# Infini-attention and GEGLU on one core: four stack tiles of a kind in place of five, two slots more, another order

## The chip, the cores and the metric

The kernel runs on one core of a Trainium2 chip. A core has engines that each work through a queue of their own, in order: TensorE (PE, matrix products, with its weight loads, PEld), VectorE (DVE), ScalarE (ACT), GpSimd (POOL), and SyncE (SP), which here issues nearly all transfers (DMA). They wait for each other by semaphores. Products are written to PSUM, eight banks of 128 partitions by 512 floats; everything else lives in SBUF or in DRAM.

The metric is the device time of one execution in microseconds (us), as the median of several runs. A verdict of faster or slower is given at 2%.

## The reference, cut

`x` is 2048 rows of 512 floats. Attention has 32 heads of 16 columns, in four segments of 512 rows; a memory `M`, `z` is carried from segment to segment. Then comes a feed-forward part of width 1376. All is float32.

```python
def _A_ref(x, wq, wk, wv, wo, beta):
    ...
    for s in range(N):                                   # N = 4 segments
        qs, ks, vs = q[:, :, s], k[:, :, s], v[:, :, s]
        logits = einsum("bhqd,bhkd->bhqk", qs, ks) * scale + mask   # causal
        a_dot = einsum("bhqk,bhkd->bhqd", softmax(logits), vs)
        pq = phi(qs)                                     # t > 0 ? t + 1 : exp(t)
        num, den = pq @ M, pq @ z + 1e-6
        outs.append(g * num / den + (1.0 - g) * a_dot)   # g = sigmoid(beta), one per head
        pk = phi(ks)
        M, z = M + pk.T @ vs, z + sum(pk)
    return concat(outs) @ wo

def _B_ref(x, w_gate, w_up, w_down):
    return (gelu(x @ w_gate) * (x @ w_up)) @ w_down

h  = x + _A_ref(layernorm(x), wq, wk, wv, wo, beta)
h2 = h + _B_ref(layernorm(h), w_gate, w_up, w_down)
```

## The kernel before

**Two halves of each number.** Operands of the large products are split into a high part in the PE's rounded format and the rest, and three products of the parts stand for one (`SPLIT`). A tile with both parts is [128, 2, 512] and is called a *slot*. Slots hold split weights (`split_weight`, `split_wv`), the transposed normalized rows, the projections before they are spread out (`hls` in `qkv`), the attention's output, and in the feed-forward part its weights and activations. One pool, `S4`, has 18 of them.

**Units and stacks.** The attention works by 16 units U, each a group of eight heads (`c`) in a segment (`s`); each unit has two halves, Q = 2U and 2U + 1, so Q runs from 0 to 31. `qkv(U)` projects q and k for a unit (`project`, L932), writes high and low part to a slot (ACT L1043, DVE L1045), and copies them with six transfers per half, three for q and three for k, into the *stacks*: a tile `stq` and a tile `stk` for each Q, in which every head takes four rows (lines 1056 and 1062 issue the copies). In a stack of K, a row of ones remains from the fill; in a stack of Q, one row of each four holds zeros at first, and later the row maxima that `pass_a` finds.

`pass_a(Q)` multiplies Q by K for the row maxima (PE L1186, DVE L1196), turns them and writes them into the stack (transfer at L1224). `pass_b(Q)` multiplies again (L1244), takes the exponential on ACT (L1250), masks on POOL (L1258) and multiplies by V (`accum`, L1272). After the last L1244 of a Q its two stacks are free. They come from pools that hand out tiles in the order of the units, five of each kind:

```python
S4 = Pool_(slots("slot", 18))
stk_t = slots("stk", 5)
PSK = Pool_(stk_t, fifo=True, then=S4)
stq_t = slots("stq", 5)
PSQ = Pool_(stq_t, fifo=True, then=S4)
```

`then=S4` says that a stack that no later Q needs becomes a slot. So 28 tiles of this size are shared by all.

Stacks are filled once on POOL: those of Q with zeros (`c_fill`, L645), those of K with ones (`c_stk`, L660). The first five Q take tiles that were so filled; from the sixth on, a transfer of 16 KB (`dst.t[3:P:32]` from `amask`, L1069) clears the row that the maxima of the tile's last user were in.

**PE's three ways of working.** Products of q, k and of most of the attention use 64 rows of the array at a time, two at once (mode "r" in the code); products by V and those with the memory use 32 columns, four at once (mode "c"); the first projection and the feed-forward part use the whole array (mode "f").

**After the attention** each segment's output is multiplied by `wo` (L1352 for two segments, L1345 for two) and normalized (`ln2`), and the feed-forward part runs in two passes of 1024 rows over 11 blocks of its width: `ffn` (L1531, activations in `geglu`) and `down` (L1596, added up by DVE at L1604). In `geglu` the low half of the result is made by POOL, and for block 9 by DVE (L1563).

**The order.** Every operation is recorded by `Sched.op` with the engine that runs it, its reads and writes, and is numbered as it is recorded. `Sched.run(ORDER)` then emits them in the sequence of a list, `ORDER`, one number for each operation. The list sets the order on each engine's queue, and which tile each value gets: a pool gives the tile that comes free first by the planner's estimate. A later operation on an engine never passes an earlier one.

At the start, POOL fills a stack, makes the identity (L629 to L633) and later the iotas of the head mask (L612, L616). PE warms up with 14 transposes (L869) once the identity and the first rows are there; then come the transposes of the first segment (L894), the first projection (L953), and V's (L994).

Of the kernel before, what the change touches and what calls it, by code (L numbers as in the profile page):

```python
# [7 lines left out]
F32 = mybir.dt.float32  # L8
# [48 lines left out]
    76, 0, 5, 9, 6, 1, 10, 12, 4, 7, 13, 14, 8, 16, 27, 11, 91, 18, 92, 88, 93, 15, 17, 89, 19, 77, 28, 94, 29,  # L57
    167, 30, 25, 90, 21, 23, 20, 31, 102, 821, 33, 97, 46, 822, 47, 103, 104, 32, 95, 22, 34, 825, 44, 87, 35,
    36, 24, 168, 105, 37, 42, 106, 164, 107, 110, 826, 38, 108, 827, 40, 96, 26, 82, 111, 100, 43, 828, 84, 98,
    39, 41, 109, 118, 128, 45, 81, 824, 48, 51, 50, 829, 119, 165, 830, 831, 112, 130, 99, 113, 823, 129, 114,  # L60
    115, 1608, 116, 117, 133, 134, 78, 120, 140, 121, 122, 49, 138, 169, 166, 52, 832, 124, 53, 123, 139, 144,
    127, 833, 834, 2, 835, 54, 135, 85, 55, 75, 131, 3, 132, 145, 1026, 146, 136, 137, 147, 150, 149, 148, 170,
    56, 181, 58, 253, 172, 634, 1024, 186, 254, 255, 151, 171, 256, 59, 57, 176, 1028, 184, 185, 188, 126, 182,
    190, 125, 187, 101, 141, 142, 189, 152, 257, 154, 74, 162, 143, 183, 153, 177, 179, 60, 836, 258, 178, 173,
    61, 180, 1029, 175, 67, 68, 1025, 174, 837, 62, 63, 191, 625, 192, 259, 631, 65, 64, 69, 260, 79, 70, 66,
    193, 194, 195, 197, 71, 72, 198, 632, 261, 73, 213, 214, 262, 161, 270, 196, 263, 838, 272, 199, 273, 438,
    2986, 628, 158, 264, 268, 839, 439, 267, 239, 240, 241, 242, 440, 215, 243, 274, 269, 271, 229, 230, 232,
    276, 441, 840, 86, 275, 233, 442, 217, 216, 203, 224, 227, 225, 228, 226, 277, 266, 443, 231, 279, 234, 265,
    83, 237, 204, 235, 238, 205, 206, 236, 444, 1030, 841, 278, 200, 202, 445, 157, 1031, 207, 245, 842, 446,
    248, 449, 208, 246, 201, 843, 209, 450, 212, 448, 211, 633, 210, 244, 249, 247, 635, 218, 155, 250, 280,  # L70
    447, 1032, 219, 220, 221, 844, 222, 163, 845, 156, 846, 251, 847, 292, 848, 1033, 849, 295, 406, 286, 1034,
    407, 281, 296, 287, 852, 1035, 223, 282, 293, 297, 288, 408, 299, 318, 850, 300, 298, 301, 409, 410, 283,
    319, 80, 289, 321, 294, 328, 291, 329, 290, 302, 1027, 411, 304, 636, 303, 306, 313, 159, 331, 305, 307,
    412, 316, 314, 361, 362, 363, 364, 365, 323, 308, 324, 326, 626, 332, 317, 413, 320, 353, 354, 355, 366,
    367, 368, 369, 370, 414, 327, 797, 322, 818, 1036, 315, 427, 428, 1417, 309, 310, 330, 815, 311, 312, 798,
    415, 432, 325, 434, 627, 356, 357, 358, 359, 360, 433, 252, 417, 418, 799, 416, 334, 335, 421, 422, 800,
    419, 801, 337, 333, 338, 336, 284, 339, 429, 430, 431, 420, 629, 630, 387, 1037, 285, 340, 390, 391, 350,
    351, 352, 371, 372, 388, 802, 377, 160, 380, 378, 379, 803, 392, 435, 398, 393, 395, 425, 804, 401, 436,
    396, 373, 375, 341, 374, 376, 437, 805, 399, 809, 482, 483, 484, 485, 486, 426, 808, 586, 342, 424, 806,
    389, 477, 478, 479, 480, 481, 394, 423, 587, 1038, 807, 382, 383, 384, 343, 1411, 381, 402, 2122, 466, 467,  # L80
    468, 588, 514, 385, 386, 515, 516, 517, 589, 344, 819, 1039, 345, 346, 503, 506, 504, 469, 470, 471, 397,
    493, 590, 472, 473, 474, 475, 476, 603, 607, 400, 591, 494, 496, 498, 592, 508, 820, 499, 501, 495, 511,
    505, 593, 541, 542, 497, 487, 347, 509, 543, 594, 816, 488, 781, 500, 544, 545, 518, 536, 512, 540, 608,
    510, 2113, 538, 489, 490, 507, 491, 492, 595, 1040, 609, 403, 502, 457, 539, 537, 614, 615, 596, 513, 519,
    1224, 613, 610, 458, 611, 404, 1041, 533, 1225, 612, 597, 520, 598, 1042, 817, 578, 600, 581, 602, 601, 534,
    521, 405, 535, 599, 1226, 567, 530, 579, 570, 568, 1227, 562, 571, 606, 563, 565, 546, 531, 1228, 532, 547,
    616, 1229, 548, 572, 580, 564, 573, 618, 604, 575, 348, 550, 649, 549, 582, 551, 552, 651, 617, 1230, 557,
    650, 560, 558, 1043, 767, 662, 664, 768, 553, 665, 555, 663, 554, 1231, 1420, 666, 522, 646, 648, 1418, 605,
    1232, 576, 657, 647, 661, 574, 660, 769, 652, 556, 659, 1233, 770, 1235, 656, 459, 1234, 658, 771, 566,
    1236, 654, 673, 851, 1414, 1044, 561, 1045, 569, 653, 674, 559, 577, 676, 583, 584, 683, 655, 772, 460, 524,  # L90
    525, 688, 773, 684, 678, 675, 677, 774, 686, 1046, 689, 1047, 667, 691, 685, 668, 681, 669, 1048, 679, 1049,
    1050, 1051, 1052, 727, 671, 690, 728, 729, 731, 670, 349, 775, 730, 776, 692, 694, 777, 461, 680, 717, 672,
    695, 718, 697, 779, 526, 721, 719, 786, 787, 792, 791, 795, 788, 687, 682, 693, 793, 720, 780, 637, 698,
    696, 699, 451, 462, 789, 700, 453, 778, 796, 638, 722, 790, 724, 723, 853, 1609, 726, 463, 464, 465, 989,
    452, 738, 701, 990, 794, 725, 585, 739, 741, 714, 743, 715, 744, 716, 746, 991, 753, 756, 1054, 740, 711,
    992, 619, 713, 993, 745, 742, 871, 527, 523, 873, 784, 872, 1003, 754, 755, 712, 994, 759, 621, 1419, 783,
    995, 879, 1056, 762, 620, 880, 760, 732, 782, 748, 749, 881, 751, 882, 996, 874, 702, 2119, 733, 875, 734,
    736, 735, 757, 876, 997, 737, 750, 883, 998, 854, 877, 752, 747, 855, 878, 1010, 999, 884, 1011, 785, 761,
    887, 528, 758, 1191, 885, 886, 1610, 763, 888, 868, 856, 1008, 1009, 869, 1012, 1053, 859, 639, 1192, 1004,
    1000, 703, 860, 622, 764, 1421, 857, 1055, 623, 765, 870, 858, 1193, 895, 1007, 898, 899, 1194, 1013, 896,  # L100
    897, 1195, 949, 1422, 950, 1006, 952, 910, 1018, 889, 913, 914, 951, 911, 890, 912, 1014, 953, 1001, 529,
    1017, 900, 901, 1015, 902, 704, 1196, 1002, 903, 904, 905, 705, 936, 908, 909, 906, 907, 1197, 1005, 1016,
    916, 919, 938, 1198, 917, 937, 918, 944, 891, 945, 892, 948, 946, 893, 947, 894, 1199, 1200, 861, 939, 862,
    1201, 810, 1213, 920, 863, 940, 941, 811, 1214, 454, 812, 1202, 864, 455, 866, 943, 1215, 706, 915, 766,
    865, 813, 867, 942, 1412, 707, 1216, 921, 922, 1203, 923, 814, 1217, 1082, 1083, 1586, 1084, 1086, 1219,
    1085, 975, 1204, 1587, 976, 977, 1218, 624, 978, 979, 933, 708, 934, 1588, 960, 961, 962, 963, 964, 935,
    954, 1205, 924, 955, 1589, 981, 1087, 982, 1208, 984, 709, 1605, 965, 966, 967, 968, 969, 1590, 1207, 1090,
    1089, 1591, 1088, 970, 1222, 971, 972, 973, 974, 1091, 1071, 1073, 1072, 1592, 1077, 1078, 1079, 956, 957,
    958, 926, 1080, 1220, 1593, 1221, 1206, 1074, 1146, 1081, 1075, 1594, 927, 1150, 1076, 1149, 1147, 1415,
    1597, 983, 1413, 1148, 985, 980, 1596, 1092, 1243, 959, 986, 1598, 1093, 1094, 1595, 1141, 987, 1095, 1096,  # L110
    1223, 925, 1209, 1019, 1020, 456, 1244, 1210, 640, 1021, 1245, 1113, 1116, 1142, 1143, 1372, 1145, 1117,
    1144, 1114, 1108, 1135, 1111, 1137, 988, 1136, 1373, 1097, 1416, 1098, 1268, 1109, 1271, 1099, 1212, 1270,
    1374, 710, 1211, 1272, 1119, 1269, 928, 1375, 1101, 1103, 641, 1120, 1376, 1121, 1122, 1102, 1104, 1138,
    1377, 642, 643, 1139, 1162, 1123, 1106, 1606, 1378, 1140, 644, 1165, 1151, 645, 1163, 1100, 1152, 1105,
    1107, 929, 1607, 1389, 1167, 1112, 1379, 1170, 2995, 1110, 1115, 1172, 1168, 1153, 1171, 1154, 1169, 1255,
    1166, 1164, 1380, 1175, 1155, 1258, 1257, 1256, 1383, 1173, 1259, 1384, 1118, 1381, 1394, 1260, 1156, 1157,
    1158, 1177, 1261, 2989, 1174, 1159, 1160, 1385, 1124, 1161, 1176, 1382, 1246, 1262, 1180, 1125, 1181, 1252,
    1126, 1253, 1057, 1058, 1183, 1391, 1392, 1178, 1393, 1179, 1254, 1396, 1022, 930, 1184, 2307, 1186, 1023,
    1059, 1263, 1395, 1127, 1387, 1294, 1397, 1187, 1295, 1185, 1266, 1182, 1267, 1296, 1060, 3183, 1297, 1062,
# [1579 lines left out]
```

## Time and profile before

| | |
|---|---|
| median of 3 runs | 746.7 us (745.68 to 749.15) |
| the profiled execution | 746.94 us, of which its span is 745.2 us |
| granted TensorE clock in it | 1.0 |
| transfers | 107.92 MB, 145 GB/s on average |

The span goes from the first to the last instruction. A row of the list of groups gives line, engine, operation, output and inputs by tile name, shape and count, then busy time and mean length, then the idle time of the engine just before, with what ended it. A row of a timeline gives start and length, and [idle time and what ended it] where the engine had waited. PE's lengths overlap, since its products are pipelined: the distance from one start to the next is what a product costs.

### The profile page before, as it was taken

To read this page: it belongs to the slowest core of one execution; us is meant where nothing else is said; L and a number is where in the kernel's file an instruction comes from. 1 tells how busy PE (TensorE), PEld (TensorE's weight loads), DVE (VectorE), ACT (ScalarE), POOL (GpSimd) and SP (SyncE) were. 2 spreads that over 40 slices of the span, in tenths; PEclk is the share of its full clock that TensorE was granted. 3 is DMA by queue.
4 is the path that set the end of the run, shared out by engine and by line. 5 is a ranking of instruction groups with operands and counts; after the bars stand their busy time and mean duration, and the time that the engine had idled before them with its cause. 6 is when DMAs were issued, how large, how long until landed. Compare 5 with 4: busy or idle time off the path is not lost.

```text
span 745.2 us, 18708 instructions
## 1 busy us (share of the span) xinstructions
PE 729.3 (98%) x6496; PEld 582.5 (78%) x6496; DVE 568.5 (76%) x1812; ACT 511.5 (69%) x1078; POOL 474.5 (64%) x750
## 2 busy tenths in 40 slices
PE   7999999999999999999999999999999999999998
PEld 6887867777877777876768788888887878888886
DVE  6897879988887898899987547775688756565466
ACT  6898888797767878878676557755586453553641
POOL 5455425564536546876884887868797578659930
PEclk9999999999999999999999999999999999999999
DMA  7756647656657757776756685554334260000003
GB/s 268 203 142 163 173 127 190 177 131 189 175 155 206 211 155 200 185 219 197 194 186 219 215 258 158 108 134 103 106 106 129 67 210 19 0 1 1 0 1 113
DMA packets 89658, 107.92 MB, mean 145 GB/s; under 512 B 31468, under 2 KB 41884, under 8 KB 89564
## 3 DMA queue, kind: packets, MB, share of 16 engines
q1 hardware_dynamic: 89260, 106.34, 50.2%
q8 instruction: 51, 0.84, 0.5%
q10 hardware_dynamic: 304, 0.39, 0.2%
q14 instruction: 43, 0.35, 0.2%
HBM read 57.03 MB, written 23.53 MB: 108 GB/s over the span
## 4 chain that ended last, share of the span: by engine, by line
PE 86%; DVE 8%; ACT 2%; issue 2%; DMA 1%; SPq 0%; DVEq 0%; ACTq 0%
PE bank L1531 28%; PE bank L1596 15%; PE bank L932 9%; PE bank L1272 8%; PE bank L1244 6%; PE bank L1186 5%; PE bank L981 5%; PE bank L1352 3%; PE bank L1345 3%; DVE bank L1196 2%; DVE aside L1196 2%; PE bank L1154 1%; DMA row<-wq 1%; DVE nm L1196 1%; PE bank L798 1%
## 5 line engine op out<-in xcount | busy, mean ns | idle before, releaser
L1250 ACT ACTIVATE row<-bank 128x512 f32<-128x512 f32 x309 | 165.5, 604 | 29.8 <-PE bank L1244 25.4
L1258 POOL TENSOR_SCALAR_AFFINE_SELECT row<-row 128x256 f32<-128x256 f32 (+1 forms) x309 | 105.9, 367 | 89.9 <-ACT row L1250 87.6
L1196 DVE CUSTOM_DVE_ANT_0 aside<-bank,amask 128x384 f32<-128x384 f32 (+2 forms) x384 | 141.7, 419 | 17.4 <-PE bank L1186 10.2
L932 PE MATMUL bank<-slot,slot 64*128 64x512 f32 x720 | 114.3, 403 | 0.0
L1531 PE MATMUL bank<-slot,slot 128*128 128x512 f32 (+1 forms) x399 | 106.1, 391 | 0.0
L1196 DVE CUSTOM_DVE_ANT_0 bank<-bank,amask 128x512 f32<-128x512 f32 x128 | 86.5, 710 | 12.0 <-PE bank L1186 10.1
L1531 PEld LDWEIGHTS bank<-slot,slot 128*128 128x128 f32 (+1 forms) x399 | 73.6, 186 | 17.5 <-issue 0.4
L1501 POOL TENSOR_TENSOR slot<-row,slot 128x512 fp32r<-128x512 f32 (+2 forms) x55 | 61.6, 1125 | 39.9 <-ACT slot L1499 37.6
L1186 PE MATMUL bank<-stk,stq 64*128 64x512 f32 (+3 forms) x512 | 82.0, 331 | 2.6 <-DMA stq<-slot 0.9
L1244 PE MATMUL bank<-stq,stk 64*128 64x384 f32 (+3 forms) x512 | 81.4, 333 | 1.7 <-DVE nm L1196 0.8
L1604 DVE TENSOR_TENSOR row<-row,bank 128x512 f32<-128x512 f32 (+1 forms) x91 | 60.4, 677 | 29.6 <-PE bank L1596 29.2
L1272 PE MATMUL bank<-row,vaug 128*32 128x512 f32 (+3 forms) x988 | 78.8, 436 | 1.2 <-DVE z L1145 0.4
L932 PEld LDWEIGHTS bank<-slot,slot 64*128 64x128 f32 x720 | 73.0, 185 | 6.2 <-DVE nm L1196 0.7
L1186 PEld LDWEIGHTS bank<-stk,stq 64*128 64x128 f32 x512 | 56.5, 185 | 14.4 <-DVE nm L1196 3.7
L1244 PEld LDWEIGHTS bank<-stq,stk 64*128 64x128 f32 x512 | 56.1, 185 | 14.6 <-DVE nm L1196 3.7
L1596 PE MATMUL bank<-slot,slot 128*128 128x512 f32 (+1 forms) x228 | 59.8, 389 | 0.0
L1272 PEld LDWEIGHTS bank<-row,vaug 128*32 128x32 f32 x988 | 30.5, 109 | 34.3 <-issue 27.3
L1531 PE MATMUL bank<-stk,slot 128*128 128x512 f32 (+1 forms) x198 | 54.7, 389 | 0.0
L981 PE MATMUL bank<-slot,slot 64*128 64x256 f32 x672 | 53.4, 284 | 0.0
L672 POOL TENSOR_TENSOR slot<-row,slot 128x512 fp32r<-128x512 f32 (+1 forms) x33 | 42.6, 1293 | 16.0 <-ACT slot L667 15.8
L1538 ACT ACTIVATE row<-bank 128x512 f32<-128x512 f32 (+1 forms) x54 | 31.6, 594 | 28.3 <-PE bank L1531 27.3
L1196 DVE DVE_READ_ACCUMULATOR2_ANT nm<- 128x1 f32 x512 | 50.1, 98 | 0.0
(269 smaller groups left out, 1622.4 us busy)
## 6 DMA issues: line engine op xcount, KB each, us to landing
stq<-slot SPq DMA_DIRECT2D x96, 128.0 KB
stk<-slot SPq DMA_DIRECT2D x94, 128.0 KB
row<-x SPq DMA_DIRECT2D x31, 256.0 KB
pv_dram<-row SPq DMA_DIRECT2D x31, 256.0 KB
row<-r_dram SPq DMA_DIRECT2D x27, 256.0 KB
row<-h_dram SPq DMA_DIRECT2D x23, 256.0 KB
row<-wd SPq DMA_DIRECT2D x17, 256.0 KB
row<-wu SPq DMA_DIRECT2D x16, 256.0 KB
```

The lines of the kernel that those rows point to most:

```text
L932: return nc.tensor.matmul(pm[i].t, w[i].t[rows_of(r), wi, dc * P:(dc + 1) * P], XT[s][dc].t[rows_of(r), xi, :], start=(dc, wi, xi, ph) == ...
L981: return nc.tensor.matmul(pms[n].t[:, 256 * t:256 * t + 256], XT[s][dc].t[rows_of(r), xi, t0:t0 + P], whl[wi].t[rows_of(r), dc // 2, 256 * ...
L1186: nc.tensor.matmul(sa.t[:, c0:c0 + w], sq.t[own, p, i * P:(i + 1) * P], sk.t[own, p, 0:w], start=True, stop=True, tile_position=(64 * a, 0 ...
L1196: nc.vector.tensor_tensor_reduce(out=(sa.t[:, c0:c0 + w] if i > 2 else aside[:, turns[0]:turns[0] + w]), in0=sa.t[:, c0:c0 + w], in1=amask ...
L1244: nc.tensor.matmul(sc.t[:, c0:c0 + D - q0], sk.t[own, p, q0:q0 + P], sq.t[own, p, q0:D], start=True, stop=True, tile_position=(64 * a, 0), ...
L1250: act(w, prio, lambda sc=sc, e=e: nc.scalar.activation(e.t[:, :w], sc.t[:, :w], AF.Exp), [sc, vtab], [e])
L1258: nc.gpsimd.affine_select(v, v, pattern=pat + [[1, P]], compare_op=OP.is_ge, fill=0.0, base=0, channel_multiplier=-1)
L1272: nc.tensor.matmul(pv.t[32 * n:32 * n + 32, kb * P:D], va.t[:, 136 * kb + 17 * j:136 * kb + 17 * j + 32], e.t[:, lo:lo + D - kb * P], star ...
L1501: pool(0.14 + 2.13e-3 * (hi - lo), prio, lambda: nc.gpsimd.tensor_tensor(v.t[:, 1, :hi - lo], r.t[:, lo:hi], v.t[:, 0, :hi - lo].bitcast(F ...
L1531: nc.tensor.matmul(dst.t[:w], v.t[:, wi, c0 + j * w:c0 + (j + 1) * w], b[bk][j].t[:, xi, :], start=first and j == 0 and n == 0, stop=j == ...
L1596: nc.tensor.matmul(pm.t[:, cs], HH[p, f, s].t[:w, hi, t * P:(t + 1) * P], v.t[:w, wi, cs], start=f == fl[0] and n == 0, stop=f == fl[-1] a ...
L1604: dve(W_, prio, lambda a=a, pm=pm, cs=cs, to=to: nc.vector.tensor_tensor(to.t[:, cs], a.t[:, cs], pm.t[:, cs], op=OP.add), [pm, a], [to])
```

## The change

There are four tiles for the stacks of Q and four for those of K, and 20 slots. The sum is 28 as before. With that, one fill of a K stack (`c_stk(4, ...)`) and one of a Q stack (`c_fill` goes over the tiles that there are) go away, and the copy that clears a used Q stack begins with Q = 4 in place of Q = 5, as its condition is `Q >= len(stq_t)`. There are 4838 operations in place of 4839: two fewer on POOL, one more on SP, and as many as before on PE (1247), DVE (1189) and ACT (1046).

The list `ORDER` is another one throughout, and its numbers stand for other operations from the missing ones on, as they are numbered when recorded. Decoded to the operations that they mean, PE's two sequences have 753 of 1247 operations in the same relative order, ACT's 628 of 1046, DVE's 807 of 1189, POOL's 435 and SP's 241. The median operation moves by 1 to 3 places on its engine.

Line 1563's operation is recorded with a mode "L" for block 9. `Sched.run` reads the mode of PE's operations alone.

```diff
 ORDER = [
-    76, 0, 5, 9, 6, 1, 10, 12, 4, 7, 13, 14, 8, 16, 27, 11, 91, 18, 92, 88, 93, 15, 17, 89, 19, 77, 28, 94, 29,
...
+    4805, 4830, 4832, 4834, 4835,
 ]
...
-    S4 = Pool_(slots("slot", 18))
+    S4 = Pool_(slots("slot", 20))
     FIN = PBL = PXT = PW = PWV = PHL = POT = PHH = S4
-    stk_t = slots("stk", 5)
+    stk_t = slots("stk", 4)
     PSK = Pool_(stk_t, fifo=True, then=S4)
-    stq_t = slots("stq", 5)
+    stq_t = slots("stq", 4)
     PSQ = Pool_(stq_t, fifo=True, then=S4)
...
         if U == 0:
             c_stk(2, [vcalm[1]])
             c_stk(3, [vcalm[1]])
-            c_stk(4, [vcalm[1]])
...
             lo(1.23 if f != 9 else D, prio, lambda: eng.tensor_tensor(
-                hh.t[:w, 1], e.t[:w], hh.t[:w, 0].bitcast(F32), op=OP.subtract), [e], [hh])
+                hh.t[:w, 1], e.t[:w], hh.t[:w, 0].bitcast(F32), op=OP.subtract), [e], [hh], mode=None if f != 9 else 'L')
```

518 rows, old and new, of the table ORDER are left out of this document.

## The prediction

> **What bounds the kernel now.** I read the page first, its chain next, then the table of windows, and then single stretches in order of time. The page says that TensorE (PE) is busy nearly all the time, and that no other engine is near it.
>
> ```profile
> span 745.2 us, 18708 instructions
> PE 729.3 (98%) x6496; PEld 582.5 (78%) x6496; DVE 568.5 (76%) x1812; ACT 511.5 (69%) x1078; POOL 474.5 (64%) x750
> PE 86%; DVE 8%; ACT 2%; issue 2%; DMA 1%; SPq 0%; DVEq 0%; ACTq 0%
> ```
>
> The chain that ended last runs on PE for 86%, so the time is that of PE's queue. Next, by stage: one window of the attention and one of the feed-forward part (columns: window, length, busy time and count of PE, PEld, DVE, ACT, POOL, granted clock, DMA share, GB/s).
>
> ```profile
> 250.00:300.00 50.00, 48.83 (x650) 37.92 (x648) 44.23 (x197) 39.52 (x89) 28.70 (x66) 1.00 0.66 180
> 500.00:550.00 50.00, 50.00 (x223) 41.40 (x222) 30.59 (x48) 34.01 (x65) 40.36 (x40) 1.00 0.44 114
> ```
>
> Both look full. The chain and the groups by line show that only the second is.
>
> ```profile
> 641.58 21.77 PE bank L1531 x96
> 58.77 1.86 PE bank L1272 x24
> 322.32 2.29 PE bank L1272 x32
> L932 PE MATMUL bank<-slot,slot 64*128 64x512 f32 x720 | 114.3, 403 | 0.0
> L1186 PE MATMUL bank<-stk,stq 64*128 64x512 f32 (+3 forms) x512 | 82.0, 331 | 2.6 <-DMA stq<-slot 0.9
> L1244 PE MATMUL bank<-stq,stk 64*128 64x384 f32 (+3 forms) x512 | 81.4, 333 | 1.7 <-DVE nm L1196 0.8
> L981 PE MATMUL bank<-slot,slot 64*128 64x256 f32 x672 | 53.4, 284 | 0.0
> L1352 PE MATMUL bank<-slot,slot 64*128 64x512 f32 x192 | 28.3, 398 | 0.0
> ```
>
> In the feed-forward part 96 matmuls of 512 columns take 21.77 us, 0.2268 each, and 223 of those are 50.6 us: that stage streams without a gap, and no order can shorten it. In the attention (from about 24 to 376 us, 352 us) the 64-row matmuls run two at a time. At the same pitch per pair the groups would need: L932 360 x 0.2268 = 81.6; L1352 96 x 0.2268 = 21.8; L981 336 x 0.1134 = 38.1; L1186 and L1244, a quarter each of 512, 384, 256 and 128 columns, 64 pairs of each form, 36.3 a line, 72.6; L1272 32 times the 2.29 of its 32 instructions less a switch (0.16, below), 68.2. The sum is 282. The 70 us left hold the small transposes and memory products, the switches of PE's tiling (some 80, 14 us, below) and waits that the busy share hides: 56 us of small work and waits together. That is the pot from which a new order can take, or to which it can add.
>
> [...]
>
> **The change, part by part.** *Two fills less.* One memset of a Q stack and one of a K stack go from POOL.
>
> ```profile
> L645 POOL MEMSET stq<- x5: 952/953/957, 0.8 to 44.9; 128x1024 f32 x5
> L660 POOL MEMSET stk<- x5: 953/955/964, 13.7 to 44.0; 128x1024 f32 x5
> L1069 SPq DMA_DIRECT2D stq<-amask x27: 534/581/602, 67.1 to 342.6; - x27
> 20.00:60.00 40.00, 38.60 (x490) 32.86 (x492) 36.69 (x171) 36.42 (x85) 19.34 (x48) 1.00 0.58 162
> ```
>
> Both lie near 44 us, where POOL is busy for 19.34 us of 40; its idle time hides them: 0 (at most -1.9, if each had held the work behind it). *One copy more.* The fifth Q stack (Q = 4) now takes a used tile, so line 1069 clears its rows: 28 copies in place of 27, 0.58 us of SyncE's (SP's) issue, ahead of the copies that use the tile; 0, or +0.6 if SP is late there.
>
> *Switches.* Decoding both lists of ORDER into operations, PE goes 83 times from one tiling to another in before, 87 in after: two round trips more between 64-row pairs and 32-column products. A round trip is seen here:
>
> ```profile
> 119.13 0.96 PE L932 MATMUL bank<-slot,slot 64*128 64x512 f32 x6
> 120.02 0.46 PE L1097 MATMUL bank<-vaug,row 128*32 128x34 f32 x32
> 120.30 0.66 PE L1272 MATMUL bank<-row,vaug 128*32 128x256 f32 x8
> 120.89 0.97 PE L932 MATMUL bank<-slot,slot 64*128 64x512 f32 x6
> 121.92 0.85 PE L932 MATMUL bank<-slot,slot 64*128 64x512 f32 x6
> 122.61 0.40 PE L1186 MATMUL bank<-stk,stq 64*128 64x256 f32 x4
> ```
>
> Six of L932 followed by their own kind of tiling take 122.61 - 121.92 = 0.69, but 120.02 - 119.13 = 0.89 ahead of a switch: 0.20. The eight of L1272 are 2.29 - 1.86 = 0.43 and take 120.89 - 120.30 = 0.59: 0.16 back. Two round trips: 2 x 0.36 = +0.7 (0 if they fall into waits, +1.4 if each meets one).
>
> *Start.* In the new list POOL begins with the iotas (L612, L616) and fills a Q stack ahead of the identity, on which PE's warm-up (L869) waits; and PE does all four groups of transposes (L894) ahead of the first projection (L953).
>
> ```profile
> 0.80 0.95 POOL L645 MEMSET stq<- 128x1024 f32 x1 [0.29 <-POOLq L1691]
> 1.73 0.21 POOL L629 MEMSET ident<- 128x128 f32 x1
> 2.65 0.46 POOL L633 TENSOR_TENSOR one<-one,ident 128x1 f32<-128x1 f32 x2
> 20.01 0.36 POOL L612 IOTA row<- 128x136 f32 x1
> 20.32 1.52 POOL L616 IOTA row<- 32x136 f32 x4
> 3.90 0.37 PE L869 MATMUL bank<-ident,row 128*24 128x128 f32 x1 [3.90 <-DMA row<-x]
> 9.91 1.35 PE L953 MATMUL bank<-slot,slot 128*128 128x256 f32 x9 [0.35 <-DVE slot L675]
> 11.89 4.96 PE L953 MATMUL bank<-slot,slot 128*128 128x256 f32 x38
> ```
>
> The identity ends at 0.80 + 1.83 (iotas, 20.01 to 21.84) + 0.95 (fill) + 1.38 (1.73 to 3.11) = 5.0, so the warm-up starts at about 5.1, 1.2 later. Most of it is absorbed, as PE waits now too (0.35 for L675, and before that for rows): 48 projections at 4.96/38 = 0.13 end at 16.9 (now 11.89 + 4.96 = 16.85) if they begin at 10.7. That is where I put the end of the last transposes: row 3 is normalized a little earlier than now, since the second half's statistics go ahead of other DVE work. I take +0.4, bounds 0 and +1.2.
>
> *Four stacks of a kind.* A stack of Q is filled by copies from a slot, is read by pass_a (L1186) and pass_b (L1244), and is free after the last of pass_b. With five, the copies for Q wait on pass_b(Q-5), with four on pass_b(Q-4).
>
> ```profile
> L1056 SPq DMA_DIRECT2D stq<-slot x96: 527/592/2082, 18.8 to 361.8; - x96
> 20.27 3.15 DMA stq<-slot
> PE bank L1186 <- DMA stq<-slot: 0.9, 1, 0.9
> ```
>
> Seven copies of 0.59 are 4.1 us of issue, and the chain shows 3.15 from the last issue until PE goes on: 7.3 us from a free tile to its use. Counted in PE work at the pitches above, the new list leaves between that release and pass_a(Q) 15.0 us on average, and least for Q = 24 (7.5), 27 (8.1), 12 and 25 (9.1) and 19 (9.2); the old one with five leaves 10.5 at least. So nothing is late if SP is free, and 0.2 to 1.9 us are spare at five places. I take +0.5, bounds 0 and +5.5 (rival B).
>
> *Two more slots.* Slots hold split weights, transposed rows and results. No wait of PE in the trace is put down to a slot that comes free; what two more allow lies in the order, next.
>
> *The order.* One place can be named. In the feed-forward part the only PE wait is this:
>
> ```profile
> 568.37 1.84 DVE L1563 TENSOR_TENSOR slot<-row,slot 128x512 fp32r<-128x512 f32 x1
> 570.13 0.67 DVE L1604 TENSOR_TENSOR row<-row,bank 128x512 f32<-128x512 f32 x1
> 570.95 0.93 PE L1531 MATMUL bank<-stq,slot 128*128 128x512 f32 x3 [0.64 <-DVE row L1604]
> ```
>
> DVE's subtraction took 1.84 us where its neighbours take 0.67, and L1604, which frees a bank, came late. The new list has three other DVE operations between the two and other PE work around them: -0.6, or 0 if another bank is then late. (The mark "L" on line 1563 changes nothing that is run: only PE's operations have their mode read.) The rest is spread over the attention. PE's two lists share 753 of 1247 operations in the same relative order; the median move is 2 places, so each wait is drawn anew. Followed through the other engines at their durations, 439 PE operations of before have their last input ready less than 1.5 us of PE work ahead, and 421 of after: 4% fewer. Taking 4% of the 56 us: -2.3. From both sides: a tenth of the pot, -5.6 and +5.6.
>
> *Sum:* 0.7 + 0.4 + 0.5 - 0.6 - 2.3 = -1.3 us. The profiled execution took 746.9 with its 745.2 of span, and the median of the runs is 746.7, so it is an ordinary run: 746.7 - 1.3 = **745.4 us**. A measurement of this kernel tells about 0.5% from no change (3.7 us: below 743.0 and above 750.4).
>
> **Rivals.** *A, the waits go broadly.* With two slots more, weights are split and rows transposed earlier, and a tenth of the pot goes: 746.7 + 0.7 + 0.4 + 0.5 - 0.6 - 5.6 = 742.1, or down to 740 if the start and the stacks cost nothing and 1.2 more of the pot goes. For it: nearly every wait is redrawn, fewer inputs are close. Against it: DVE is busy 44 of 50 us in the attention and keeps its work, and the four switches are added.
>
> *B, the refill of the stacks is late: slower.* SP issues in order, and a wait ahead of a copy holds all copies behind it.
>
> ```profile
> SPq L1224 <- ACT slot L1043: 12.4, 3, 9.0
> SPq L814 <- DVE vaug L812: 9.0, 2, 6.9
> ```
>
> If SP is held for 2.5 us when a tile comes free, the refill needs 9.8 instead of 7.3, and the five places named above, with 8.6 on average, lose 1.2 each, 6 us: 746.7 + 0.7 + 0.4 - 0.6 + 6 - 2.3 = 750.9; held for longer, more. It decides from 7.5 - 7.3 = 0.2 us of holding at the tightest place and from 1.9 at all five. For it: SP does wait that long. Against it: those waits are mostly elsewhere, and 23 of the 28 refills have more than 9.2 us.
>
> [...]
>
> *C, nothing is changed that PE sees.* The switches, the start and the pot cancel: 746 to 748.
>
> **How the numbers follow.** My forecast and C end within 0.5%: together 0.52 (0.32 and 0.20). A and what goes beyond it: 0.28. B and a start or switches at their upper ends: 0.20. The range must leave out no more than 0.2: it goes from 740.0, below A, to 751.5, above B at 2.5 us. The likeliest case's own range is 743.0 to 748.5. Faster 0.28, same 0.52, slower 0.20.
>
> **What would show it.** In the profile after: PE's first matmul near 5.1 us rather than 3.9; L953 ending near 17; no PE wait on L1604; 8 stack fills; PE still streaming 96 matmuls in 21.77 us; PE's waits ended by "DMA stq<-slot" or "DMA stk<-slot" under 1.5 us in all. If those waits come to 3 us or more, B is right. If the feed-forward part begins over 3 us earlier or later, I have mis-sized the pot; if it takes another time from there to the end, I am wrong that it has no room.

## The result, and the profile after

| kernel | median of the runs, us | ratio to before, 95% interval |
|---|---|---|
| before | 746.59 (745.68 to 749.15, 6 runs) | |
| after | 751.87 (750.14 to 752.58, 6 runs) | 1.0061 (1.0044 to 1.0077) |
| after, a second time (e10, beside other runs of before) | 753.18 (750.77 to 753.92, 6 runs) | 1.0082 (1.0062 to 1.0101) |

The change makes the kernel slower, by 5.3 and 7.1 us in the medians and by 4.6 and 6.1 in the ratios. That is under the 2% at which a verdict of slower is given, but clear of no change: both intervals lie above 1. I had forecast 745.4, range 740.0 to 751.5: the sign was wrong, and the time is 0.4 beyond the upper end. After's profiled execution took 752.6 us, with a span of 750.8 against 745.2.

Ahead of its groups the page of after has, as the page of before:

```profile
span 750.8 us, 18743 instructions
PE 734.6 (98%) x6496; PEld 585.2 (78%) x6496; DVE 568.6 (76%) x1812; ACT 511.0 (68%) x1078; POOL 474.0 (63%) x748
```

PE does the same 6496 matmuls and is busy 5.3 us longer; every other engine does the work it did. "Busy" hides the loss here: PE's idle time is 15.9 us in before and 16.2 in after, so nearly all of it lies in what counts as busy. So I take a landmark, the output projection L1352, whose last matmul is nearly the end of the attention. The view of that line's instructions in before, then in after (count, duration min/median/max in ns, first and last start):

```profile
L1352 PE MATMUL bank<-slot,slot x192: 383/392/496, 310.4 to 375.2; 64*128 64x512 f32 x192
```

```profile
L1352 PE MATMUL bank<-slot,slot x192: 383/392/496, 312.3 to 380.4; 64*128 64x512 f32 x192
```

At the first L1352 after is 1.9 us late, at the last 5.2. What follows changes little: the spans are 5.6 apart. The feed-forward part is as I had described it: its window is full, and its only wait is 0.29 where it was 0.64. The windows of after, as those quoted of before, then that wait in the timeline:

```profile
250.00:300.00 50.00, 49.31 (x646) 36.65 (x642) 43.67 (x193) 38.18 (x85) 28.16 (x65) 1.00 0.70 186
500.00:550.00 50.00, 49.94 (x221) 40.96 (x220) 29.16 (x47) 28.87 (x55) 37.58 (x39) 1.00 0.45 111
```

```profile
574.45 0.96 PE L1530 MATMUL bank<-stq,slot 128*128 128x512 f32 x3 [0.29 <-DVE row L1603]
```

The first window of after is even a little fuller than that of before (49.31 against 48.83), although PE loses time there: the busy share of a window can't be used for this. The start of after:

```profile
4.33 0.39 PE L869 MATMUL bank<-ident,row 128*24 128x128 f32 x1 [4.33 <-POOL ident L630]
7.60 1.28 PE L894 MATMUL bank<-ident,row 128*128 128x128 f32 x8 [0.25 <-ACT row L889]
11.21 6.02 PE L953 MATMUL bank<-slot,slot 128*128 128x256 f32 x48 [0.61 <-ACT slot L899]
17.07 5.92 PE L994 MATMUL bank<-slot,slot 128*128 128x256 f32 x48
```

L994 follows at 17.07; in before it is 0.4 earlier:

```profile
16.68 5.92 PE L994 MATMUL bank<-slot,slot 128*128 128x256 f32 x48
```

At the first L932, the start of the attention's products, nothing is left of that. Before, then after:

```profile
24.06 0.94 PE L932 MATMUL bank<-slot,slot 64*128 64x512 f32 x6
24.02 0.94 PE L932 MATMUL bank<-slot,slot 64*128 64x512 f32 x6
```

So the loss is in the attention. The place where most of it comes at once is near 350 us; DVE's timeline, then PE's:

```profile
346.23 3.20 DVE L789 TENSOR_SCALAR row<-row,mv,ln 128x512 f32<-128x512 f32 x4
349.36 0.55 DVE L1196 CUSTOM_DVE_ANT_0 aside<-bank,amask 128x384 f32<-128x384 f32 x1
```

```profile
348.79 0.73 PE L1186 MATMUL bank<-stk,stq 64*128 64x256 f32 x5
350.66 0.49 PE L1186 MATMUL bank<-stk,stq 64*128 64x512 f32 x1 [1.14 <-DVE nm L1196]
```

Four normalizations of the second layer norm (L789) stand in a row on DVE; the row maxima (L1196) behind them read banks, and PE's next scores need one of these. In before the four lie between maxima (0.91, 0.54 and 0.99 for two):

```profile
342.20 0.91 DVE L789 TENSOR_SCALAR row<-row,mv,ln 128x512 f32<-128x512 f32 x1
343.94 0.54 DVE L789 TENSOR_SCALAR row<-row,mv,ln 128x512 f32<-128x512 f32 x1
344.87 0.99 DVE L789 TENSOR_SCALAR row<-row,mv,ln 128x512 f32<-128x512 f32 x2
```

**Two theories.** *Theory 1:* the new order makes PE wait longer for banks that DVE's row maxima still have to read; the block above is the largest piece, the others are small. *Theory 2* is rival B of the prediction: the four stacks are refilled too late.

### The profile page after: what moved, and what is told of

It reads as the page before. It is cut to its first block, busy times and chain, and to the rows that moved or that the text cites. A ratio compares the mean times of both kernels' runs of the same rounds, so it can differ in the third digit from the quotient of the medians.

```text
span 750.8 us, 18743 instructions
## 1 busy us (share of the span) xinstructions
PE 734.6 (98%) x6496; PEld 585.2 (78%) x6496; DVE 568.6 (76%) x1812; ACT 511.0 (68%) x1078; POOL 474.0 (63%) x748
## 4 chain that ended last, share of the span: by engine, by line
PE 56%; DVE 4%; ACT 1%; POOL 1%; issue 1%; DMA 0%; SPq 0%; DVEq 0%; ACTq 0%; POOLq 0%
PE bank L1530 27%; PE bank L1595 16%; PE bank L1272 3%; PE bank L1345 3%; PE bank L932 2%; PE bank L1352 2%; PE bank L1186 1%; PE bank L1244 1%; DVE aside L1196 1%; DVE bank L1196 1%; POOL row L1258 1%; PE bank L981 0%; ACT row L1250 0%; DMA stq<-slot 0%; PE bank L1154 0%
## 5 line engine op out<-in xcount | busy, mean ns | idle before, releaser
L1196 DVE CUSTOM_DVE_ANT_0 aside<-bank,amask 128x384 f32<-128x384 f32 (+2 forms) x384 | 142.1, 419 | 22.0 <-PE bank L1186 11.6
L1530 PE MATMUL bank<-slot,slot 128*128 128x512 f32 (+1 forms) x447 | 117.9, 390 | 0.0
L932 PE MATMUL bank<-slot,slot 64*128 64x512 f32 x720 | 113.5, 404 | 0.3 <-DVE nm L1196 0.2
L1530 PEld LDWEIGHTS bank<-slot,slot 128*128 128x128 f32 (+1 forms) x447 | 82.5, 185 | 19.1 <-ACT vaug L1250 0.3
L1196 DVE CUSTOM_DVE_ANT_0 bank<-bank,amask 128x512 f32<-128x512 f32 x128 | 86.0, 710 | 6.9 <-PE bank L1186 6.3
L1603 DVE TENSOR_TENSOR row<-row,bank 128x512 f32<-128x512 f32 (+1 forms) x85 | 56.1, 677 | 33.6 <-PE bank L1595 33.5
L1272 PE MATMUL bank<-row,vaug 128*32 128x512 f32 (+3 forms) x992 | 80.0, 443 | 1.3 <-DVE nm L1196 0.6
L932 PEld LDWEIGHTS bank<-slot,slot 64*128 64x128 f32 x720 | 73.7, 185 | 6.1 <-DVE nm L1196 1.7
L1500 POOL TENSOR_TENSOR slot<-row,slot 128x512 fp32r<-128x512 f32 (+3 forms) x56 | 61.4, 1101 | 26.2 <-ACT slot L1498 20.9
L1595 PE MATMUL bank<-slot,slot 128*128 128x512 f32 (+1 forms) x264 | 68.0, 390 | 0.1
L1244 PEld LDWEIGHTS bank<-stq,stk 64*128 64x128 f32 x512 | 54.2, 184 | 16.8 <-DVE nm L1196 4.7
L1272 PEld LDWEIGHTS bank<-row,vaug 128*32 128x32 f32 x992 | 31.4, 111 | 38.4 <-issue 32.1
L1595 PEld LDWEIGHTS bank<-slot,slot 128*128 128x128 f32 (+1 forms) x264 | 49.4, 188 | 10.9 <-DVE row L1603 0.5
L1562 POOL TENSOR_TENSOR slot<-row,slot 128x512 fp32r<-128x512 f32 (+1 forms) x27 | 34.9, 1295 | 26.1 <-ACT slot L1559 26.1
L1196 DVE DVE_READ_ACCUMULATOR2_ANT nm<- 128x1 f32 x512 | 50.0, 98 | 0.1
```

What stands on the lines that cost most here:

```text
L932: return nc.tensor.matmul(pm[i].t, w[i].t[rows_of(r), wi, dc * P:(dc + 1) * P], XT[s][dc].t[rows_of(r), xi, :], start=(dc, wi, xi, ph) == ...
L1196: nc.vector.tensor_tensor_reduce(out=(sa.t[:, c0:c0 + w] if i > 2 else aside[:, turns[0]:turns[0] + w]), in0=sa.t[:, c0:c0 + w], in1=amask ...
L1244: nc.tensor.matmul(sc.t[:, c0:c0 + D - q0], sk.t[own, p, q0:q0 + P], sq.t[own, p, q0:D], start=True, stop=True, tile_position=(64 * a, 0), ...
L1272: nc.tensor.matmul(pv.t[32 * n:32 * n + 32, kb * P:D], va.t[:, 136 * kb + 17 * j:136 * kb + 17 * j + 32], e.t[:, lo:lo + D - kb * P], star ...
L1500: pool(0.14 + 2.13e-3 * (hi - lo), prio, lambda: nc.gpsimd.tensor_tensor(v.t[:, 1, :hi - lo], r.t[:, lo:hi], v.t[:, 0, :hi - lo].bitcast(F ...
L1530: nc.tensor.matmul(dst.t[:w], v.t[:, wi, c0 + j * w:c0 + (j + 1) * w], b[bk][j].t[:, xi, :], start=first and j == 0 and n == 0, stop=j == ...
```

## The experiments

In e1 to e4 the code lines stand two lower than in after, since their lists of the order take fewer lines; in e5 to e7 they stand three or four higher than in before and after, by the lines that were put in. "Last L1352" is the landmark from above (before 375.2, after 380.4).

**e1: the pools alone, and e2 to e4: one place of the new order each**

e1 is before with the new pools. PE, ACT, DVE and POOL keep their lists (less the two fills); on SP copies into stacks stand later, behind work that they preceded (95 of the 218, if all other operations of the list are counted).

```diff
-    S4 = Pool_(slots("slot", 18))
+    S4 = Pool_(slots("slot", 20))
-    stk_t = slots("stk", 5)
+    stk_t = slots("stk", 4)
-    stq_t = slots("stq", 5)
+    stq_t = slots("stq", 4)
```

> The pools of after (20 slots, four stacks of Q, four of K) with the order of before: PE, ACT, DVE and POOL keep before's order (less the two fills that are gone), and on SP 73 of the 218 copies into stacks go back as far as the fewer tiles make them. Theory 1 (the loss lies in the new order, mainly where DVE does four of L789 in a row near 346 us, PE then waits for L1196, and the granted clock falls to 0.5): as before, 745.5 to 748.5 us, no clock of 0.5 ahead of the end. Theory 2 (rival B: four stacks are refilled too late): 750 us or more, with PE waits on stq<-slot or stk<-slot of 3 us or more.

Measured: 773.30 us, ratio 1.035 (1.0328 to 1.0373); last L1352 at 401.0. PE's timeline has waits on refills that neither before nor after has:

```profile
254.66 0.50 PE L1242 MATMUL bank<-stq,stk 64*128 64x512 f32 x2 [3.35 <-DMA stq<-mx]
288.14 1.33 PE L1184 MATMUL bank<-stk,stq 64*128 64x384 f32 x6 [3.81 <-DMA stq<-slot]
329.98 0.50 PE L1184 MATMUL bank<-stk,stq 64*128 64x384 f32 x4 [4.20 <-DMA stk<-slot]
```

Theory 1 as I had written it misses: one stack less of each kind costs 26 us where the order isn't made for it. (At most 7 us of these are the clock: the mean granted clock was 0.991, and 0.009 of 771 us is 6.9.) The new order takes back 21 of them. Whether what is left is still the refill has to be asked separately (e5).

e2 changes DVE's list in one place, the four L789 (operations 3065 to 3068; 2735 and the like are row maxima, 2807 and 2794 are L1045):

```diff
- 3065, 3067, 3066, 3068, 2735, 2738, 2737, 2736, 2807, 2748, 2730, 2746, 2794
+ 3065, 3067, 2735, 2738, 2737, 2736, 2807, 3066, 2748, 2730, 2746, 3068, 2794
```

> After, with DVE's order changed in one place alone: of the four L789 near 346 us two stay ahead of the first L1196 group, one goes behind that group, one behind the next. Theory 1: PE's wait of 1.14 us on L1196 near 350 us shrinks to under 0.3, the clock stays at 1.0 from 348 to 358 us, and the kernel gains 1.5 (the wait) to 3.4 us (with the clock): 748.5 to 750.5 us. Theory 2: no change, 751.4 to 752.4 us. A third (the clock falls there for another reason): the wait goes and the clock falls all the same, 750.4 to 751 us.

Measured: 750.52 us, ratio 1.005 (1.0036 to 1.0065), last L1352 at 379.0: 1.4 us of the 5.2 come back in the trace. The wait of 1.14 is gone, but two smaller ones come behind it, and the clock falls there (0.54 from 356 to 358 us, 0.61 from 358 to 360). That is the third case of the expectation:

```profile
353.68 0.50 PE L1184 MATMUL bank<-stk,stq 64*128 64x384 f32 x3 [0.69 <-DVE nm L1194]
355.73 0.44 PE L1242 MATMUL bank<-stq,stk 64*128 64x384 f32 x2 [0.25 <-ACT row L1248]
```

So the block is a piece of the loss, and not most of it.

e3 changes POOL's list in one place (2383 is L1311, 2384 is L1313):

```diff
- 2605, 2694, 2383, 2607, 2384, 2697, 2704, 2702, 2699, 2713, 2715, 3291, 3292, 2757
+ 2605, 2694, 2607, 2697, 2704, 2702, 2699, 2713, 2715, 3291, 3292, 2383, 2384, 2757
```

> After, with POOL's order changed in one place alone: L1311 and L1313 (1.29 and 1.45 us), which run beside the four L789 near 346 us, go behind L1507 near 352 us. If the four L789 are slow (0.80 us each) because POOL works beside them, they take 0.55 to 0.70 each, the block ends 0.4 to 1 us earlier, PE's wait of 1.14 us on L1196 shrinks by as much, and the kernel gains 0.4 to 1 us, or up to 2.8 if the clock then stays at 1.0: 749 to 751.5 us. If their pace has nothing to do with POOL, they stay at 0.80 and so does the time, 751.4 to 752.4 us, or up to 754 through L1311's and L1313's own delay.

Measured: 754.29 us, ratio 1.0109 (1.0083 to 1.0136). The pace of L789 came out as expected from POOL; the time did not, it misses the 749 to 751.5 us that went with it and lies just over the 754 of the other case. The durations of the four L789 in after, then in e3 (there L787):

```profile
L789 DVE TENSOR_SCALAR row<-row,mv,ln x4: 536/700/1504, 346.2 to 348.9; 128x512 f32<-128x512 f32 x4
```

```profile
L787 DVE TENSOR_SCALAR row<-row,mv,ln x4: 447/582/631, 350.7 to 352.1; 128x512 f32<-128x512 f32 x4
```

The longest, 1504 ns, is the one that lies over POOL's L1313; without it none takes over 631. But the results of L1311 and L1313 are stored by SP in its order: that store is issued at 357.45 us, in after at 348.72, and the next copies into stacks at 358.57 instead of 349.84. PE then waits for stacks (this profile's execution, of 759.4 us, is the slowest of the six):

```profile
367.34 0.74 PE L1184 MATMUL bank<-stk,stq 64*128 64x512 f32 x6 [1.45 <-DMA stk<-slot]
369.54 0.80 PE L1242 MATMUL bank<-stq,stk 64*128 64x512 f32 x2 [1.46 <-DMA stq<-mx]
```

That is rival B's mechanism, at a place where after itself stays clear of it.

e4 puts operation 4 (the identity) at the head of POOL's list (2 are the iotas, 76 a fill):

```diff
- 2, 0, 76, 4, 99, 92
+ 4, 2, 0, 76, 99, 92
```

> After, with POOL's order changed at the start alone: the identity goes ahead of the iotas and of the first fill, as in before. My step (start, +0.4 us) says that PE's first matmul goes back from 4.33 to 3.9 us and the kernel gains 0.4 us: 751.2 to 751.7. If the rows' arrival sets the first projection, the first matmul moves and L953 still ends at 17.1 us: no change, 751.6 to 752.2.

Measured: 752.76 us, ratio 1.0084 (1.0067 to 1.0101): no gain. PE begins earlier and gets nothing for it:

```profile
3.78 0.37 PE L867 MATMUL bank<-ident,row 128*24 128x128 f32 x1 [3.78 <-DMA row<-x]
18.26 1.96 PE L992 MATMUL bank<-slot,slot 128*128 128x256 f32 x15
```

V's projections begin at 18.26 here, at 17.07 in after's first profile and at 17.93 in its second, with the same order of the rest. In the two late ones DVE's statistics (L864, here L862) wait for rows of x twice more, 0.44 and 0.30 us here and 0.44 and 0.32 there; the first profile has no such waits. So the arrival of the rows decides, and the start varies by about 1 us between executions.

**e5, e6, e7: the refills sent elsewhere**

```diff
-                                              hl.t[64 * h:64 * h + 64, part].bitcast(F32)),
+                                              hl.t[64 * h:64 * h + 64, part].bitcast(F32)) if Q < 4 else
+                            nc.sync.dma_start(dump[Q][0][r], hl.t[64 * h:64 * h + 64, part].bitcast(F32)),
```

The same is done for the copies into K stacks and from amask; dump is a place in DRAM for each copy. In e7 it begins at Q = 5.

> After, in its own order, with the refills of the stacks sent elsewhere: for Q from 4 on the copies from a slot (and the one from amask) go to a place of their own in DRAM, so SP issues as many transfers of the same size, but none waits for a stack that comes free and PE waits for none of them; the scores are computed from the first fill's contents, so this part of the result is left out. Theory 1 (the rest of the loss is waits on DVE, ACT and POOL as the new order draws them): the waits on stq<-slot and stk<-slot go (0.4 to 1.6 us near 283), all else stays, 750 to 751.7 us. Theory 2 (refills that come late hold after back, seen or through what they push): 747 us or less.

> The run with before's order and the new pools (773.3 us), with the refills sent to DRAM in the same way from Q = 4 on; that part of the result is left out. If its 26 us over before are refills that come late, nearly all of it goes: 746 to 750 us. If SP's other order or something else of the pools made it, 760 us or more.

> Before, with the refills sent to DRAM in the same way from Q = 5 on (five stacks are filled first); that part of the result is left out. It shows what refills cost with five stacks. Theory 1: nothing but the 0.9 us of waits on stq<-slot, 745.5 to 747 us. Theory 2: five stacks leave room, so the gain here is under 1 us too, while after without refills gains 4 us or more.

| kernel | without refills, us | ratio to before | with refills |
|---|---|---|---|
| after (e5) | 751.35 | 1.0057 (1.0041 to 1.0074) | 1.0061 and 1.0082 |
| new pools, before's order (e6) | 748.18 | 1.0024 (1.0010 to 1.0039) | 1.035 |
| before (e7) | 746.12 | 0.9991 (0.9977 to 1.0005) | 1 |

By the ratios the refills cost 24 us in e1, 0.3 to 1.9 in after, and nothing that can be told from 0 in before. The landmark (here L1356) in e5, then in e7:

```profile
L1356 PE MATMUL bank<-slot,slot x192: 383/390/497, 311.4 to 379.5; 64*128 64x512 f32 x192
L1356 PE MATMUL bank<-slot,slot x192: 383/390/501, 309.7 to 374.6; 64*128 64x512 f32 x192
```

Without any refill to wait for, the gap is 4.9 where it was 5.2. Theory 2 falls. (The 2 us that e6 keeps over before may be SP's changed order; they were not looked into.)

**e8, e9: cheaper row maxima, in after and in before**

```diff
-  out=(sa.t[:, c0:c0 + w] if i > 2 else aside[:, turns[0]:turns[0] + w]), in0=sa.t[:, c0:c0 + w],
-  in1=amask[:, D - w:], op0=OP.add, op1=OP.min, scale=-1.0, scalar=BIG,
+  out=(sa.t[:, c0:c0 + w // 4] if i > 2 else aside[:, turns[0]:turns[0] + w // 4]), in0=sa.t[:, c0:c0 + w // 4],
+  in1=amask[:, 0:w // 4], op0=OP.add, op1=OP.min, scale=-1.0, scalar=BIG,
```

> After, in its own order, with L1196 on a quarter of its columns (128x128 in place of 128x512, and so on) and without the mask, so the row maxima are those of a quarter of the keys: that part of the result is changed. DVE loses some 150 us of its 568, and the banks that it reads come free sooner. To be read against the same edit of before. Theory 1a (the 5 us are waits on DVE's row maxima and on what stands behind them in DVE's queue, drawn anew by the order): the gap to the light before shrinks to 1.5 us or less. Theory 1b (the gap is made by the start, by ACT, POOL and the switches): it stays at 4 to 6 us.

> Before with the same edit of L1196, as the other side of that comparison. Waits on DVE are a part of the loss on PE here too, so both theories expect a gain over before; 5 to 12 us under 746.5. Theory 1a: after gains about 4 us more than this one. Theory 1b: both gain the same.

> After as it is, in the same call as the other two, for a second profile: 751 to 752.6 us. If the losses are in the order, they stand at the same places in this profile: near 275 to 287 and 347 to 356 us; a clock of 0.5 that is set by PE's wait of 1.14 us near 350 comes again behind it.

Measured: after 740.55 us, ratio 0.9923 (0.9904 to 0.9942); before 739.93, ratio 0.9902 (0.988 to 0.9924); after unchanged, beside them, 753.18. The light before and the light after differ by 0.6 us in the medians and by 1.6, with about 2 either way, in the ratios, where the full ones differ by 5.3 and 7.1 in the medians and by 4.6 and 6.1 in the ratios. The landmark says the same; the light before, then the light after:

```profile
L1352 PE MATMUL bank<-slot,slot x192: 383/390/478, 304.1 to 367.9; 64*128 64x512 f32 x192
```

```profile
L1352 PE MATMUL bank<-slot,slot x192: 383/390/494, 304.5 to 368.3; 64*128 64x512 f32 x192
```

Late by 0.4 at the first L1352 and by 0.4 at the last, instead of 1.9 and 5.2. A part of this is chance: in its profile the light before has half clock near the start.

```profile
12.00:14.00 2.00, 2.00 (x12) 2.00 (x11) 0.13 (x1) 1.27 (x5) 1.93 (x4) 0.50 1.05 387
```

So the fair stretch is from the first L932, in the light before, then in the light after:

```profile
25.77 0.95 PE L932 MATMUL bank<-slot,slot 64*128 64x512 f32 x6
25.20 0.94 PE L932 MATMUL bank<-slot,slot 64*128 64x512 f32 x6
```

From there to the last L1352 the light before takes 342.1 us and the light after 343.1, the full ones 351.1 and 356.4: 1.0 instead of 5.2. After's second profile (e10) has its losses where the first has them, and its last L1352 at 381.7:

```profile
352.06 0.50 PE L1186 MATMUL bank<-stk,stq 64*128 64x512 f32 x1 [1.41 <-DVE nm L1196]
```

So some 4 of the 5.2 us hang on DVE's row maxima and what queues with them. The rest, about 1 us, is what the start, the switches, ACT and POOL add with a lighter DVE; DVE's spare time may also have absorbed a part of what they add in the full kernels. PE's own waits on the row maxima show a part of the loss, where PE stood idle; in before, then in after (total us, times, longest):

```profile
PE bank L1244 <- DVE nm L1196: 0.8, 2, 0.5
PE bank L1272 <- DVE nm L1196: 0.2, 1, 0.2
PE bank L1097 <- DVE nm L1196: 0.2, 1, 0.2
```

```profile
PE bank L1186 <- DVE nm L1196: 1.5, 2, 1.1
PE bank L1272 <- DVE nm L1196: 0.6, 3, 0.2
PE bank L1244 <- DVE nm L1196: 0.4, 1, 0.4
PE bank L932 <- DVE nm L1196: 0.2, 1, 0.2
PE bank L1097 <- DVE nm L1196: 0.2, 1, 0.2
```

1.2 against 2.9 us; in the light ones it is 0.7 and 0.5. Other waits of PE fell by about as much, as its idle time shows, so this alone proves little.

The traces allow a fuller count. In the five traces no PE matmul begins sooner than 0.05 us after another engine's last read of its bank has ended, and many begin 0.05 to 0.08 us after: I take these to have waited for it. So each delay of a PE operation (over 0.1 us behind the pitch of the operation ahead of it, from 24 us to the last L1352) can be put to what ended it. The sums in us, estimates from the starts and ends in the five traces:

| delays of PE's operations | before | after | after (e10) | light before | light after |
|---|---|---|---|---|---|
| all | 43.0 | 48.2 | 49.7 | 34.8 | 35.8 |
| for a bank that DVE had to read | 18.6 | 22.9 | 22.4 | 3.7 | 3.7 |
| of these, by a row maximum (L1196) | 13.4 | 16.4 | 16.2 | 0.1 | 1.4 |
| for a bank that ACT had to read | 3.0 | 3.8 | 4.3 | 6.7 | 7.3 |
| for an input | 0.2 | 0.7 | 1.1 | 1.1 | 0.3 |
| at a switch, or put to nothing | 21.2 | 20.9 | 21.8 | 23.3 | 24.5 |

Some 4 us of the growth are at banks that DVE had to read (3.5 to 5.0 with other choices of the pitch and of the 0.1 us), and there the light pair is even. Both light kernels beat both originals, but they find the maxima of a quarter of the keys, which only bounds the exponents as long as the other scores are not much larger: a measurement, not a version to ship.

**e11, e12, e13: can small moves in the order take it back?**

Each is made of many small moves within the engines' lists, which together shift an operation by at most 6 places on PE and 14 on DVE; e11 in after, e12 in before, both anywhere ahead of the feed-forward part (163 and 177 places of PE's list, 568 and 553 of DVE's differ), e13 in after between 225 and 300 us alone (59 of PE's, 128 of DVE's). The first of e13's moves on PE and on DVE, as a sample:

```diff
- 1672, 2287, 1428, 1687, 2288, 1598, 2289, 1684, 2290, 1601, 1779
+ 1672, 1428, 2287, 1687, 2288, 1598, 2289, 1684, 2290, 1779, 1601
- 1698, 1699, 1766, 1753, 1430, 1429, 1689, 1240, 1688, 1686
+ 1698, 1766, 1699, 1240, 1753, 1430, 1429, 1688, 1689, 1686
```

> After's pools and work, with its order changed by many small moves of up to five places within each engine's list, ahead of the feed-forward part, chosen so that PE waits less for DVE, ACT and POOL at the durations that the traces show (L789, L1146 and L1563 as slow as they ran). If the 5 us are only how this order draws PE's waits, they can be moved out again by such small moves: 744 to 748.5 us, before's time or better. If four stacks and 20 slots force them (too little room between one pass_b and the next pass_a), it stays at 750 us or more.

> Before's pools, with its order changed by the same kind of small moves, as the other side. If both kernels hold about as much that such moves can take out, this one gains as much as the other: 740 to 744.5 us, and the gap of some 5 us between the two pools stays. If before's order was merely the luckier draw and the pools are worth the same, the two come out within 2 us of each other.

> After, with such moves in one stretch alone, from about 225 to 300 us, which the traces name as the place of 2.5 to 3 us of the loss (waits of 0.3 to 0.6 us for banks that DVE reads). If so, this stretch takes 1.5 to 2.5 us less and the rest is as in after: 749 to 750.8 us. If the loss there comes from elsewhere, 751.4 us or more.

Measured: 758.27 us (ratio 1.0161, 1.0137 to 1.0186), 750.43 (1.0049, 1.003 to 1.0068) and 751.06 (1.006, 1.0038 to 1.0083). None gains what was hoped for. e11 lies in the second case of its expectation in the number alone: e12 misses both of its cases, so the moves cost time in either order. Moves that should have saved several us by the durations of the traces cost 6 us in after and 4 in before. A part may be switches of tiling, 94 in e11's list of PE where after's has 87, and 85 in e12's where before's has 83. A part of e11's may be the clock: its median run has 0.995, and its one run at 1.000 took 755.5 us. e13, aimed at one stretch and with 87 switches, falls between the two cases of its expectation, near where after lies. PE's waits in e11 name what was given up:

```profile
PE bank L1186 <- DMA stk<-slot: 1.2, 1, 1.2
PE bank L798 <- DVE row L789: 0.7, 1, 0.7
PE bank L1244 <- DVE row L967: 0.6, 1, 0.6
```

These sets of moves didn't mend the order; e2's single one took 1.4 us out in the trace. So it stays open whether four stacks of a kind force these waits on the row maxima, by bringing pass_a of one Q close behind pass_b of another, or whether this order merely drew them. The new order was not run with five stacks of a kind.

## Why the prediction was wrong, step by step

The prediction split 1.0 us of fixed terms (0.7 + 0.4 + 0.5 - 0.6) from the "pot" of attention waits, of which it took 2.3 away.

- **Fills and the copy more, 0:** right. The page counts four fills of each kind, and POOL's 748 instructions are two fewer.
- **Start, +0.4:** right in size at L994 (17.07 against 16.68), but the reason only half, and the 16.9 against 16.85 of my own sum would have given 0.1. PE could begin at 4.3, not 5.1, since it waits for L630 alone, and my sum ran on to the three L633 behind it. L953 ends at 17.2. At the first L932 nothing is left of the loss in the first profile (24.02 against 24.06); in the second L994 begins at 17.93. e4 shows that the identity is not what decides.
- **Switches, +0.7:** not to be told apart. They remain in e8 and e9, where all that is left of the gap from the first L932 on is 1.0.
- **Refill, +0.5, bounds 0 and 5.5:** right in size. e5 puts it at 0.3 to 1.9, and PE's waits on "DMA stq<-slot" are 0.7 (below the 1.5 that I had named), one wait at 23.71 for the first Q's stack, where before waits 0.92. Rival B had the sign and nearly the time (750.9), but not the cause. e1 shows how near it was: the same pools with another order cost 26 us.
- **L1563 and L1604, -0.6:** right in direction; the wait fell from 0.64 to 0.29, 0.35. The feed-forward part has no more to give, as I had said.
- **The rest of the attention, -2.3: this step failed.** It counted the PE operations whose *last input* is ready less than 1.5 us ahead (439 and 421) and turned 4% fewer into 4% less waiting. But at the waits that grew the inputs had been there for long. At 350.66 PE had what it multiplies; it lacked the bank to write to, which DVE's L1196 had not read yet. A buffer that must come free was no part of my count. In the table above the delays for a late input are 0.2 us in before and 0.7 and 1.1 in after, those for a bank that DVE had to read 18.6, and 22.9 and 22.4: some 4 of the 5 us lie where I did not look. (With each operation told apart by its number, PE's two lists share 637 of 1247 in the same relative order, not 753; the argument is the same.)

The other terms came out near their sizes, though the switches could not be measured alone, and the loss lies within the bounds that I gave for the pot; what failed is how the change draws from it. Its bounds were stated as -5.6 and +5.6, and I let only the lower one become a rival (A). With 1.0 of fixed terms and +5.6 the sum would have been 753.3, and a range up to there would have held the time. No reason in the profile excluded that side.

The line of what would show the pot mis-sized was the right test: the last L1352, ahead of the feed-forward part, is 5.2 us later.

## What to carry to other kernels

Where a new order is judged, count the buffers that have to come free as well as the inputs that have to arrive: at a wait, ask what the instruction writes to and who reads that last. If the largest unknown term can go either way, its upper end belongs into the range like its lower one. To see which engine makes a loss that is spread over many small waits, make that engine's work cheaper in both kernels and see whether the gap closes.

## What the runs showed of the hardware that was not expected

**L789 on DVE took 1504 ns over a POOL operation of 1.45 us.** The four L789 near 350 us take 447 to 631 ns in e3, where L1311 and L1313 come later; in after the longest takes 1504, with POOL's L1313 under it. Before has the like at L1563 on DVE: 1.84 us over a POOL operation of 1.28, and 0.69 with none under it. The timeline of POOL in after:

```profile
347.25 1.45 POOL L1313 TENSOR_TENSOR vaug<-vaug,row 128x512 f32<-128x512 f32 x1
```

The four L789 of after end 0.28, 0.28, 0.29 and 0.31 us after the end of the POOL operation that each lies over, and these take 1.29, 0.60, 1.45 and 0.48 us; L1563 in before ends 0.55 us after the one of 1.28. What held DVE there was not shown.

**Behind a wait of 1.14 us PE's clock was halved for 3.4 us.** The windows behind that wait in after (granted clock third from the right):

```profile
350.00:352.00 2.00, 1.26 (x7) 0.53 (x11) 2.00 (x10) 1.30 (x5) 1.92 (x6) 0.95 0.95 261
352.00:354.00 2.00, 2.00 (x16) 0.65 (x12) 2.00 (x8) 1.62 (x4) 1.09 (x3) 0.50 0.80 194
354.00:356.00 2.00, 2.00 (x26) 1.13 (x18) 1.21 (x5) 0.37 (x1) 0.71 (x1) 0.69 0.09 28
```

In steps of 0.25 us the clock is 0.50 in each from 352.00 to 355.00 and 1.00 from 355.25 on. The time at half clock is 2 x (1 - 0.95)/0.5 + 2 + 2 x (1 - 0.69)/0.5 = 3.4 us, and the 32 matmuls of L1272 there take from 351.47 to the next group at 355.45, 4.0 us, where 32 took 2.29 in before. After's second profile has half clock too, behind a wait of 1.41 (0.87 from 352 to 354 us, 0.50 from 354 to 356); e4, with a wait of 1.15 at the same place, has 1.00 from 350 to 356 us, e2 has it behind waits of 0.69 and 0.25 (0.54 and 0.61 from 356 to 360 us), and the light before near its start, behind 0.85 and 0.64 (0.50 from 12 to 14 us). So it came behind a wait of 1.14 us and not behind one of 1.15: what brings it was not shown. It is not what made after slower: after's six runs have a mean clock of 1.000 in three (751.6, 752.2, 750.1 us) and 0.998 to 0.999 in the others (752.6, 752.4, 750.5).
